# Operands moved to multiples of 512 and 1,024 bytes, and relu and square of three pairs in eight done by ScalarE

## The chip, the cores and the metric

The kernel runs on one core of a Trainium2 chip. The metric is the device time of one execution in microseconds (us); the median of three runs is given. A profile of one execution, taken by the hardware profiler, says what each engine did: PE is the matrix engine (PEld its weight loads), DVE is VectorE, ACT is ScalarE, POOL is GpSimd, and SP issues most of the transfers.

## The reference

A short causal convolution over the sequence (7 taps, softmax weights, one set for each of 8 heads) is followed by a two-layer network with an activation of three branches.

```python
def _attn_ref(x, weight):                     # x: 8 x 4096 x 192, weight: 8 x 7
    w = softmax(weight, axis=-1)
    x_pad = np.concatenate([np.zeros((B, pad, D)), x], axis=1)
    x_unf = x_pad[:, idx, :].reshape(B, S, K, H, group)
    return np.einsum('hk,bskhg->bshg', w, x_unf)

def _moe_ref(x, w_in, w_out):                 # x: 32768 x 192, w_in: 192 x 2048, w_out: 2048 x 192
    h = x @ w_in
    neg, pos = h <= -1, h >= 1
    g = np.where(pos, h, np.where(neg, 0.0, (h + 1) ** 2 / 4))
    return g @ w_out
```

## The kernel before, in words

**Tiles and steps.** The 32,768 rows are taken in 64 blocks of 512 (`s`, TB = 512), two blocks to a chunk `c`. The 2,048 hidden channels are 16 groups of 128, taken two at a time, so a block has 8 pairs (NPAIR = 8). The main loop (L830) runs over 512 pairs `q`, 8 to a block and 16 to a chunk; `i` is the pair's place in the chunk, 0 to 15. One turn of the loop is called a step here. In a step PE first does `mm1(q)`, the product with w_in for this pair, into one of two buffers `h` of PSUM, and then `mm2(q - 2)`, the product with w_out for the pair two steps back, which adds into four accumulators (`accm0`, `accm1`, `accr0`, `accr1`) that exist once.

**Precision.** From the second block on each product is made of three: weights and activations are split into a high part and a rest (`hi` and `lo`, `gh` and `gl`, type fp32r), and high by high, rest by high and high by rest are added up. Each matmul uses one half of the partitions (64 of 128), and the two halves run as a pair beside each other. `mm1` has 18 matmuls (9 pairs), `mm2` has 20 (10 pairs), so a step has 19 pairs of matmuls, all with 512 columns. The stationary operand of `mm1` and `mm2` is always 128 columns (512 bytes in a partition) of a weight tile `w2` to `w9` or `wr2` to `wr9`; the moving one is 512 columns (2,048 bytes) of an activation tile (`hi`, `lo`, `rh`, `rl`, `rhi`, `rlo`, `gh`, `gl`). The first block (s = 0) is done with plain float32 operands instead (L401 and `mm2_first`, L426), in whose products with w_out the activation is the stationary operand and 192 columns of the weights move.

**The activation.** For the pair q, `act_clip` (L460) has DVE clip h to -1 to 1 into a tile `g`, `act_square` (L466) has ACT square (g + 1) / 2 in place, and `act_max` (L471) has DVE take the larger of h and g. In the next step `act_hi` (L478) has ACT round g to `gh`, and `act_lo` (L483) has DVE subtract to `gl`. In the first block another form is in use: `both_square` (L745) has ACT do relu((h + 1) / 2) and then square it, and `most` (L752) has DVE take min(g, 1) and then the larger of that and h, in one instruction.

**Beside it.** When a block's last `mm2` has been issued, in the step with q mod 8 = 1, `evac` (L491) has ACT copy the four accumulators out; POOL adds them in pairs, and DVE transposes the sums for the store. The convolution of the next chunk runs in the same steps by a fixed plan (L697 to L705): transposes on DVE, products with the taps on ACT (`p`, `y`), their sums on POOL. Every engine takes its instructions in the order in which the program issues them; the schedule is manual.

**Where tiles stand.** Pools are laid out in each partition in the order in which they are opened, and tiles in a pool in the order in which they are first named, each rounded up to 32 bytes. The pool `const` begins at byte 16,512, which is 32 x 512 + 128. The weight tiles come first in it and all have sizes that are multiples of 512, so every weight tile starts at 128 modulo 512. Behind them come `wk` (56 bytes), `warm` (4), `whose` (1,120, of which 1,024 are used) and `ident` (512), then the pool `stage`, then `xin` with three tiles of 2,176 bytes, `xw` with two of 2,176 and five of 2,048, and then `xo`, `act` and `ob`, whose tiles are multiples of 1,024 bytes. By these sizes the tiles of `xo`, `act` and `ob`, the activations among them, all start at 448 modulo 1,024 (the first of them at byte 134,592).

Of the kernel before, what the change touches and what calls it, by code (L numbers as in the profile page):

```python
# [8 lines left out]
F32 = mybir.dt.float32  # L9
# [4 lines left out]
AF = mybir.ActivationFunctionType  # L14
# [4 lines left out]
P = 128  # L19
# [11 lines left out]
def lightconv_then_ffn(ctx: ExitStack, tc: tile.TileContext, x, weight, w_in, w_out, out):  # L31
# [24 lines left out]
    nc = tc.nc  # L56
    B, S, D = x.shape
    H, K = weight.shape
# [6 lines left out]
    NPAIR = NF // 2  # L65
# [5 lines left out]

    const = ctx.enter_context(tc.tile_pool(name="const", bufs=1))
    stage = ctx.enter_context(tc.tile_pool(name="stage", bufs=2))
    xin = ctx.enter_context(tc.tile_pool(name="xin", bufs=3))
    xw = ctx.enter_context(tc.tile_pool(name="xw", bufs=2))
    xo = ctx.enter_context(tc.tile_pool(name="xo", bufs=3))
    act = ctx.enter_context(tc.tile_pool(name="act", bufs=2))
    ob = ctx.enter_context(tc.tile_pool(name="ob", bufs=2))
    ps_h = ctx.enter_context(tc.tile_pool(name="ps_h", bufs=2, space=PSUM))
    ps_o = ctx.enter_context(tc.tile_pool(name="ps_o", bufs=1, space=PSUM))  # L80
    ctx.enter_context(tc.manual_schedule())
# [53 lines left out]
    class Conv:  # L135
# [133 lines left out]
        def split_halves(self):  # L269
# [26 lines left out]
    wo_w = w_out.bitcast(U32).rearrange("(f p) (d two) -> p f d two", p=P, two=2)  # L296
    n_in = [CI if j < NPAIR else 0 for j in range(NCH)]
    n_all = [n_in[j] + (CO if j >= LAG else 0) for j in range(NCH)]
    W = [const.tile([P, 2, n_in[j] + (CW if j >= LAG else 0)], F32R, name=f"w{j}")
         for j in range(NCH)]  # L300
    CC = max(n_all)
# [12 lines left out]
    class Chunk:  # L314
# [51 lines left out]
        def parts(self, rest):  # L366
            j, k = self.j, n_in[self.j]
            if rest:
                yield (WF[j][:, :, 0:P],
                       *(W[j][:, i, k:].rearrange("p (f d) -> p f d", f=2) for i in range(2)))  # L370
                yield WF[j][:, :, P:], WR[j][:, :, 0], WR[j][:, :, 1]
            else:
                yield WI[j], W[j][:, 0, 0:k], W[j][:, 1, 0:k]

# [11 lines left out]
    NQ = NSB * NPAIR  # L386
    WHOLE = (NF32 + 1,)
    hs, g32, gs, ghs, gls, accs = {}, {}, {}, {}, {}, {}

    def mm1(q):  # L390
# [11 lines left out]
        else:  # L402
            mms = [(W[j][:, part], u + u, [xop[s][u, x]] * 2) for u in "nsr"
                   for part, x in ((0, "hi"), (1, "hi"), (0, "lo"))]
# [25 lines left out]
    def mm2(q):  # L430

        s, j = divmod(q, NPAIR)
        gh, gl = ghs.pop(q), gls.pop(q)
        w, wr, k = W[j + LAG], WR[j + LAG], n_in[j + LAG]
        if j == 0:
# [21 lines left out]
    def tiles(q):  # L457
        return [slice(0, 1), slice(1, 2)] if q == NQ - 1 else [slice(0, 2)]

    def act_clip(q):  # L460
        g = gs[q] = act.tile([P, 2, TB], F32, name="g", bufs=3)
        for e in tiles(q):
            nc.vector.tensor_scalar(out=g[:, e, :], in0=hs[q][:, e, :], scalar1=-1.0, scalar2=1.0,  # L463
                                    op0=ALU.max, op1=ALU.min)

    def act_square(q):  # L466
        g = gs[q]
        for e in tiles(q):
            nc.scalar.activation(g[:, e, :], g[:, e, :], AF.Square, bias=0.5, scale=0.5)  # L469

    def act_max(q):  # L471
        h, g = hs.pop(q), gs[q]
        for e in tiles(q):
            nc.vector.tensor_tensor(out=g[:, e, :], in0=h[:, e, :], in1=g[:, e, :], op=ALU.max)  # L474
        if q < NF32:
            g32[q] = gs.pop(q)
# [90 lines left out]
                    in_=y[i][:, 0:2 * D].rearrange("p (b d) -> p b d", b=2))  # L567


    wk = const.tile([P, 2, K], F32, name="wk")  # L570
    warm = const.tile([P, 1], F32, name="warm")
    whose = const.tile([P, 2 * P + 3 * K + 3], F32, name="whose")[:, 0:2 * P]
    one = ob.tile([P, TB], F32, name="sum")[:, 0:P]
    small, busy = (ob.tile([P, TB // SQ, SQ], F32, name="osb").rearrange("p j b -> p (j b)")
                    for _ in range(2))
# [176 lines left out]
    def most(h, g):  # L752

        nc.vector.scalar_tensor_tensor(out=g, in0=g, scalar=1.0, in1=h, op0=ALU.min, op1=ALU.max)
# [75 lines left out]
    for q in range(NQ + DELAY):  # L830
# [22 lines left out]
        else:  # L853
# [6 lines left out]
            if q < NQ:  # L860
                let_go()
                act_clip(q)
                act_square(q)
# [6 lines left out]
            if q < NQ:  # L870
                let_go()
                act_max(q)
                parts_lo(q, (False,))
                conv_slot(i, conv_b, conv_n.get("a"), conv_n.get("r"))
# [38 lines left out]
```

## Time and profile before

| | us |
|---|---|
| median of three runs (2256.04 to 2256.80) | 2256.71 |
| span of the profiled execution, from its first instruction to its last | 2255.6 |
| what lies around the span: median less span | 1.1 |
| DVE, ACT and POOL busy in the span | 2103.2, 1697.6, 1168.4 |
| DVE busy, and ACT busy, in 16 steps in the middle (69.60 us) | 65.58, 52.88 |

The span is one execution; the median is that of other executions of the same kernel, and the two differ by what is spent before the first and after the last instruction. A busy time is the time in which an engine had an instruction in work. Idle time on an engine costs nothing as long as another one, which sets the end, does not wait for it.

### The profile page before, as it was taken

How to read it: one execution, taken by the hardware profiler on the slowest of the kernel's cores; microseconds unless marked ns; L12 is line 12 of the kernel's file. 1: busy time of each engine (PE TensorE's matmuls, PEld its weight loads, DVE VectorE, ACT ScalarE, POOL GpSimd, SP SyncE). 2: the span in 40 equal slices, each digit the busy share in tenths (PEclk: the TensorE clock that was granted, in tenths of full speed). 3: DMA queues.
4: the chain of work that ended last, by engine and by line, in shares of the span. 5: the costliest groups of instructions: out<-in, count | busy, mean ns of one | idle time of the engine just before them, and what ended most of it. 6: DMA issues, size and time to landing. Idle time of an engine off the chain costs nothing.

```text
span 2255.6 us, 48202 instructions
## 1 busy us (share of the span) xinstructions
PE 2249.6 (100%) x19645; PEld 1842.2 (82%) x19645; DVE 2103.2 (93%) x1883; ACT 1697.6 (75%) x2153; POOL 1168.4 (52%) x868
## 2 busy tenths in 40 slices
PE   9999999999999999999999999999999999999999
PEld 6988888888888888888888888888888888888887
DVE  8899999999999999999999999999999999999997
ACT  7677877778777787777877777877778777787775
POOL 1446644556445565454654455644556545565441
PEclk9999999999999999999999999999999999999999
DMA  7222222222222212222222222222222222212211
GB/s 158 49 51 48 42 46 47 51 53 39 51 49 46 53 34 51 49 49 51 41 46 47 49 51 51 39 49 46 49 53 39 51 49 46 54 35 50 49 34 24
DMA packets 442125, 110.84 MB, mean 49 GB/s; under 512 B 410288, under 2 KB 417840, under 8 KB 441904
## 3 DMA queue, kind: packets, MB, share of 16 engines
q1 hardware_dynamic: 441744, 107.66, 25.8%
q8 instruction: 155, 2.54, 0.5%
q14 instruction: 66, 0.54, 0.1%
q10 hardware_dynamic: 160, 0.10, 0.0%
HBM read 32.84 MB, written 25.17 MB: 26 GB/s over the span
## 4 chain that ended last, share of the span: by engine, by line
PE 100%; ACT 0%; DVE 0%; issue 0%; DVEq 0%; POOL 0%; POOLq 0%; ACTq 0%
PE h L408 47%; PE accm L452 30%; PE accr L452 20%; PE accr L426 1%; PE accm L426 1%; PE accr L190 0%; PE accm L602 0%; PE accr L408 0%; PE accm L181 0%; PE h L155 0%; PE h L553 0%; PE accr L646 0%; ACT xT L168 0%; ACT xT L165 0%; ACT xT L167 0%
## 5 line engine op out<-in xcount | busy, mean ns | idle before, releaser
L230 POOL TENSOR_TENSOR y<-y,p 128x512 f32<-128x512 f32 x546 | 765.5, 1402 | 730.8 <-DVE g L474 559.5
L487 DVE TENSOR_TENSOR gl<-g,gh 128x1024 fp32r<-128x1024 f32 (+1 forms) x497 | 732.1, 1473 | 27.6 <-ACT gh L481 23.6
L469 ACT ACTIVATE g<-g 128x1024 f32<-128x1024 f32 (+1 forms) x505 | 535.3, 1060 | 242.4 <-DVE g L463 232.9
L463 DVE TENSOR_SCALAR g<-h 128x1024 f32<-128x1024 f32 (+1 forms) x505 | 609.8, 1208 | 97.1 <-PE h L408 88.1
L481 ACT CAST gh<-g 128x1024 fp32r<-128x1024 f32 (+1 forms) x497 | 521.7, 1050 | 237.1 <-DVE g L474 225.6
L408 PE MATMUL h<-hi,w 64*128 64x512 f32 x4032 | 629.8, 389 | 0.0
L474 DVE TENSOR_TENSOR g<-h,g 128x1024 f32<-128x1024 f32 (+1 forms) x505 | 613.4, 1215 | 12.1 <-ACT g L469 4.5
L452 PE MATMUL accm<-gh,w 64*128 64x512 f32 x3966 | 535.0, 388 | 0.0
L408 PEld LDWEIGHTS h<-hi,w 64*128 64x128 f32 x4032 | 382.6, 184 | 81.9
L452 PEld LDWEIGHTS accm<-gh,w 64*128 64x128 f32 x3966 | 372.3, 184 | 81.8 <-issue 0.2
L408 PE MATMUL h<-lo,w 64*128 64x512 f32 x2016 | 399.6, 388 | 0.0
L219 ACT ACTIVATE p<-xT,wk 128x512 f32<-128x512 f32 x562 | 375.1, 710 | 0.0
L452 PE MATMUL accm<-gl,w 64*128 64x512 f32 x1984 | 308.1, 388 | 0.0
L452 PE MATMUL accr<-gl,wr 64*128 64x512 f32 x1984 | 308.0, 388 | 0.0
L452 PE MATMUL accr<-gh,wr 64*128 64x512 f32 x1984 | 308.0, 388 | 0.0
L408 PE MATMUL h<-rh,w 64*128 64x512 f32 x992 | 306.0, 388 | 0.0
L408 PE MATMUL h<-rhi,w 64*128 64x512 f32 x992 | 306.0, 388 | 0.0
L408 PEld LDWEIGHTS h<-lo,w 64*128 64x128 f32 x2016 | 193.3, 184 | 41.5 <-DMA lo<-lo 0.3
L501 POOL TENSOR_TENSOR sum<-t 128x512 f32<-128x512 f32 (+1 forms) x124 | 160.7, 1316 | 126.3 <-ACT t L499 126.3
L452 PEld LDWEIGHTS accm<-gl,w 64*128 64x128 f32 x1984 | 186.4, 184 | 40.9
L452 PEld LDWEIGHTS accr<-gh,wr 64*128 64x128 f32 x1984 | 186.4, 184 | 40.9
L452 PEld LDWEIGHTS accr<-gl,wr 64*128 64x128 f32 x1984 | 186.4, 184 | 40.9
(145 smaller groups left out, 1976.8 us busy)
## 6 DMA issues: line engine op xcount, KB each, us to landing
out_dram<-osb SPq DMA_DIRECT2D x366, 64.0 KB, 2.0
raw<-in_x_dram SPq DMA_DIRECT2D x334, 68.0 KB, 2.4
hi<-hi SPq DMA_DIRECT2D x126, 128.0 KB, 2.3
lo<-lo SPq DMA_DIRECT2D x126, 128.0 KB, 2.3
rhi<-rh SPq DMA_DIRECT2D x62, 128.0 KB, 2.2
rlo<-rl SPq DMA_DIRECT2D x62, 128.0 KB, 2.3
words<-in_moe_w_in_dram SPq DMA_DIRECT2D x16, 192.0 KB, 4.0
words<-in_moe_w_out_dram SPq DMA_DIRECT2D x8, 384.0 KB, 5.0
```

Source lines behind the costliest of these rows:

```text
L219: nc.scalar.mul(p, self.xT[:, SH + k:SH + k + TB], wk[:, self.wsel, k:k + 1])
L230: nc.gpsimd.tensor_add(y, y, self.product(k))
L408: nc.tensor.matmul(h[e], w[HALVES[e], c0:c0 + P], x[e][e], start=(n == 0), stop=(n == len(mms) - 1))
L426: nc.tensor.matmul(accs[s][a, i][:, c0:c0 + D], g[half, e, b * P:(b + 1) * P], w[half, e, :], start=(j == 0 and e == 0 and b % 2 == 0), st ...
L452: nc.tensor.matmul(accs[s][a, i], st, g[HALVES[i], e, :], start=(j == 0 and n == first[a]), stop=(j == NPAIR - 1 and n == last[a]))
L463: nc.vector.tensor_scalar(out=g[:, e, :], in0=hs[q][:, e, :], scalar1=-1.0, scalar2=1.0, op0=ALU.max, op1=ALU.min)
L469: nc.scalar.activation(g[:, e, :], g[:, e, :], AF.Square, bias=0.5, scale=0.5)
L474: nc.vector.tensor_tensor(out=g[:, e, :], in0=h[:, e, :], in1=g[:, e, :], op=ALU.max)
L481: nc.scalar.copy(gh[:, e, :], gs[q][:, e, :])
L487: eng.tensor_sub(gl[:, e, :], g[:, e, :], gh[:, e, :])
L501: nc.gpsimd.tensor_add(y[:, n], t[0][:, n], t[1][:, n])
```

## The change

It has two parts.

**Places.** `warm` is now the first tile of `const` and is given 320 bytes, of which the first element is used; `wk` follows (56 bytes, rounded to 64). So the weights begin at 16,512 + 320 + 64 = 16,896 = 33 x 512: every weight tile, and every slice of 128 columns that a matmul takes from it, starts at a multiple of 512. `whose` loses its padding. The pools `xw` and `xin`, whose tiles of 2,176 bytes are no multiple of 1,024, are opened last, so that `xo`, `act` and `ob` follow `stage` and all their tiles start at multiples of 1,024 (the first at 113,664 = 111 x 1,024). The tiles `xT`, `y`, `p` and `raw` of the two pools that are moved stand at multiples of 128. No instruction of PE is added, removed or moved by this.

**The activation.** For pairs with q mod 8 equal to 1, 4 or 6, from the third block to the last but one (q from 16 to 503, so 183 pairs), the form of the first block is used: ACT does relu and then square, and DVE does the one instruction of `most`. The clip on DVE goes.

```diff
     const = ctx.enter_context(tc.tile_pool(name="const", bufs=1))
     stage = ctx.enter_context(tc.tile_pool(name="stage", bufs=2))
-    xin = ctx.enter_context(tc.tile_pool(name="xin", bufs=3))
-    xw = ctx.enter_context(tc.tile_pool(name="xw", bufs=2))
     xo = ctx.enter_context(tc.tile_pool(name="xo", bufs=3))
     act = ctx.enter_context(tc.tile_pool(name="act", bufs=2))
     ob = ctx.enter_context(tc.tile_pool(name="ob", bufs=2))
+    xw = ctx.enter_context(tc.tile_pool(name="xw", bufs=2))
+    xin = ctx.enter_context(tc.tile_pool(name="xin", bufs=3))
...
+    warm = const.tile([P, 80], F32, name="warm")[:, 0:1]
+    wk = const.tile([P, 2, K], F32, name="wk")
     W = [const.tile([P, 2, n_in[j] + (CW if j >= LAG else 0)], F32R, name=f"w{j}")
          for j in range(NCH)]
...
+    def on_scalar(q):
+        return 2 * NPAIR <= q < NQ - NPAIR and q % NPAIR in (1, 4, 6)
+
     def act_clip(q):
         g = gs[q] = act.tile([P, 2, TB], F32, name="g", bufs=3)
+        if on_scalar(q):
+            nc.scalar.activation(g, hs[q], AF.Relu, bias=0.5, scale=0.5)
+            return
...
     def act_square(q):
         g = gs[q]
+        if on_scalar(q):
+            nc.scalar.activation(g, g, AF.Square)
+            return
...
     def act_max(q):
         h, g = hs.pop(q), gs[q]
+        if on_scalar(q):
+            most(h, g)
+            return
...
-    wk = const.tile([P, 2, K], F32, name="wk")
-    warm = const.tile([P, 1], F32, name="warm")
-    whose = const.tile([P, 2 * P + 3 * K + 3], F32, name="whose")[:, 0:2 * P]
+    whose = const.tile([P, 2 * P], F32, name="whose")
```

Two places show what moves. The first is ACT in the steps i = 8 and i = 9 of a chunk, up to the copies of the four accumulators. `gh<-g` is the rounding of the pair before, L248 a rounding for the convolution, L226 and L219 are products with taps. Before:

```order
L481 CAST gh<-g 128x1024
L469 ACTIVATE g<-g 128x1024
L248 CAST hi_5281<-y 128x512
L226 ACTIVATE y<-xT,wk 128x512
L219 ACTIVATE p<-xT,wk 128x512 x2
L481 CAST gh<-g 128x1024
L469 ACTIVATE g<-g 128x1024
L498 COPY t<-accm_4904 128x512
L499 COPY t<-accm_4905 128x512
L498 COPY t<-accr_4906 128x512
L499 COPY t<-accr_4907 128x512
```

In the changed kernel (its lines are numbered 8 to 14 higher here) the same place reads:

```order
L495 CAST gh<-g 128x1024
L480 ACTIVATE g<-g 128x1024
L248 CAST hi_5281<-y 128x512
L226 ACTIVATE y<-xT,wk 128x512
L219 ACTIVATE p<-xT,wk 128x512 x2
L495 CAST gh<-g 128x1024
L468 ACTIVATE g<-h 128x1024
L477 ACTIVATE g<-g 128x1024
L512 COPY t<-accm_4904 128x512
L513 COPY t<-accm_4905 128x512
L512 COPY t<-accr_4906 128x512
L513 COPY t<-accr_4907 128x512
```

The relu (L468) is new, and it stands between the rounding of g and the square, ahead of the copies that free the accumulators. The second place is DVE from the transpose that ends the step i = 7 to the transpose for the store in the step i = 10. Before:

```order
L147 STREAM_TRANSPOSE xT<-raw 128x544
L463 TENSOR_SCALAR g<-h 128x1024
L487 TENSOR_TENSOR gl<-g,gh 128x1024
L474 TENSOR_TENSOR g<-h,g 128x1024
L463 TENSOR_SCALAR g<-h 128x1024
L487 TENSOR_TENSOR gl<-g,gh 128x1024
L474 TENSOR_TENSOR g<-h,g 128x1024
L463 TENSOR_SCALAR g<-h 128x1024
L487 TENSOR_TENSOR gl<-g,gh 128x1024
L474 TENSOR_TENSOR g<-h,g 128x1024
L524 STREAM_TRANSPOSE osb<-sum 128x512
```

And in the changed kernel:

```order
L147 STREAM_TRANSPOSE xT<-raw 128x544
L471 TENSOR_SCALAR g<-h 128x1024
L501 TENSOR_TENSOR gl<-g,gh 128x1024
L488 TENSOR_TENSOR g<-h,g 128x1024
L501 TENSOR_TENSOR gl<-g,gh 128x1024
L766 SCALAR_TENSOR_TENSOR g<-g,h 128x1024
L471 TENSOR_SCALAR g<-h 128x1024
L501 TENSOR_TENSOR gl<-g,gh 128x1024
L488 TENSOR_TENSOR g<-h,g 128x1024
L538 STREAM_TRANSPOSE osb<-sum 128x512
```

In the step i = 9 the clip is gone and `most` (L766) stands where the maximum stood; the steps on either side are as they were.

## The prediction, made before the changed kernel ran

> **What bounds the kernel now.** I read the head of the page first, then the chain that ended last, then what PE waited for.
>
> ```profile
> span 2255.6 us, 48202 instructions
> PE 2249.6 (100%) x19645; PEld 1842.2 (82%) x19645; DVE 2103.2 (93%) x1883; ACT 1697.6 (75%) x2153; POOL 1168.4 (52%) x868
> PEclk9999999999999999999999999999999999999999
> PE 100%; ACT 0%; DVE 0%; issue 0%; DVEq 0%; POOL 0%; POOLq 0%; ACTq 0%
> ```
>
> PE is busy in the whole span at a full granted clock, and the chain lies on PE alone. A busy PE need not be PE at its best, so the waits of PE come next, and then the pace of its steps.
>
> ```profile
> PE accm L602 <- POOL osb L606: 1.2, 1, 1.2
> PE accr L190 <- ACT xT L168: 0.7, 1, 0.7
> PE h L553 <- DVE t L547: 0.2, 1, 0.2
> ...
> 1168.77 1.08 PE L452 MATMUL accm<-gh,w 64*128 64x512 f32 x8
> 1203.56 1.07 PE L452 MATMUL accm<-gh,w 64*128 64x512 f32 x8
> ```
>
> The three waits of PE add up to 2.1 us in all, at the two ends of the program. The two rows of the timeline are eight steps apart: 34.79 / 8 = 4.349 us a step, and with 19 pairs of matmuls in a step 0.2289 us a pair. In the main part, then, PE waits for nobody, and the time is the number of pairs times 0.2289. That number:
>
> ```profile
> L408 PE MATMUL h<-lo,w 64*128 64x512 f32 x2016 | 399.6, 388 | 0.0
> L452 PE MATMUL accr<-gl,wr 64*128 64x512 f32 x1984 | 308.0, 388 | 0.0
> ```
>
> Each of these stands four times in a step, so there are 504 steps with the new `mm1` (9 pairs) and 496 with the new `mm2` (10 pairs): 4,536 + 4,960 = 9,496 pairs, or 2,174 us of the span. What is left is the first block and the two ends.
>
> Is 0.2289 us the best a pair can do? The first block has pairs of the same shape with float32 operands, and others with 192 columns:
>
> ```profile
> 23.02 1.88 PE L408 MATMUL h<-hi,gh 64*128 64x512 f32 x8
> 24.73 1.02 PE L408 MATMUL h<-rh,gh 64*128 64x512 f32 x4
> 25.59 0.82 PE L426 MATMUL accm<-wf,g 64*128 64x192 f32 x8
> 26.24 0.82 PE L426 MATMUL accr<-wf,g 64*128 64x192 f32 x8
> ```
>
> From 23.02 to 25.59 there are six pairs of 512 columns, 0.4283 us each; from 25.59 to 26.24 four pairs of 192, 0.1625 us each. The 320 further columns cost 0.2658 us, so a column costs 0.83 ns and a pair 3 ns beside its columns. The fp32r pair takes a little over half of the float32 one. If a float32 operand costs exactly two columns' time where an fp32r one costs one (an estimate from these rows; nothing shows the two goes apart), the fp32r pair should take 512 x 0.415 + 3 = 0.2156 us. It takes 13.3 ns more, in every pair, whatever the other engines do. Over 9,496 pairs that is **126 us**.
>
> **The change part by part.** *Places.* PE's instructions stay as they are; only where their operands stand changes. So a pair's time can change only through the reading of operands, and no row of before has an fp32r pair at another place. I bound it: at best all of the 13.3 ns goes (-126 us); nothing may change (0); at worst the same excess comes a second time (+126 us). I take the first, since the nearest rows, the float32 pairs, read the same tiles without an excess, and since the excess is the same in all 19 pairs of a step, `mm1` and `mm2` alike, whose one common trait is the places: weights at 128 modulo 512, activations at 448 modulo 1,024. Against it speaks that the float32 pairs have no excess at those same places; they take twice as long over the same bytes, which would hide it.
>
> [...]
>
> *The activation.* The rows with the durations, the last three from the first block, where the new form is in use already:
>
> ```profile
> L474 DVE TENSOR_TENSOR g<-h,g 128x1024 f32<-128x1024 f32 x503 | 612.2, 1217 | 12.1 <-ACT g L469 4.5
> L463 DVE TENSOR_SCALAR g<-h 128x1024 f32<-128x1024 f32 x503 | 608.5, 1210 | 96.4 <-PE h L408 87.4
> L754 DVE SCALAR_TENSOR_TENSOR g<-g,h 128x1024 f32<-128x1024 f32 x7 | 8.5, 1215 | 0.0
> L749 ACT ACTIVATE g<-g 128x1024 f32<-128x1024 f32 x7 | 7.4, 1054 | 0.0
> L747 ACT ACTIVATE g<-h 128x1024 f32<-128x1024 f32 x7 | 7.1, 1021 | 2.3 <-PE h L408 2.3
> ...
> 1202.60:1272.20 69.60, 69.60 (x610) 57.06 (x610) 65.58 (x57) 52.88 (x66) 37.26 (x26) 1.00 0.26 47
> ```
>
> For each pair moved DVE loses the clip (1.21 us) and its other instruction costs the same; ACT gains the relu (1.02 us). Sixteen steps, 69.60 us now, hold six such pairs. With pairs of 0.2156 us they last 16 x 19 x 0.2156 = 65.5 us. DVE, busy for 65.58, would then have been the bound; it now has 65.58 - 6 x 1.21 = 58.3 (89%), and ACT 52.88 + 6 x 1.02 = 59.0 (90%). By load, both fit. By order one place is tight: the copies that free the accumulators stand behind the new relu. The rows from the end of `mm1(q)` at i = 8 to the next block's first `mm2`:
>
> ```profile
> 1168.77 1.08 PE L452 MATMUL accm<-gh,w 64*128 64x512 f32 x8
> 1168.97 1.22 DVE L463 TENSOR_SCALAR g<-h 128x1024 f32<-128x1024 f32 x1
> 1170.23 1.06 ACT L469 ACTIVATE g<-g 128x1024 f32<-128x1024 f32 x1 [0.88 <-DVE g L463]
> ...
> 1172.33 1.32 ACT L219 ACTIVATE p<-xT,wk 128x512 f32<-128x512 f32 x2
> 1173.56 1.04 ACT L481 CAST gh<-g 128x1024 fp32r<-128x1024 f32 x1
> 1174.58 1.06 ACT L469 ACTIVATE g<-g 128x1024 f32<-128x1024 f32 x1
> 1175.55 0.56 ACT L498 COPY t<-accm 128x512 f32<-128x512 f32 x1
> 1176.01 0.59 ACT L499 COPY t<-accm 128x512 f32<-128x512 f32 x1
> ...
> 1177.24 0.87 PEld L452 LDWEIGHTS accm<-gh,w 64*128 64x128 f32 x8
> 1177.47 1.07 PE L452 MATMUL accm<-gh,w 64*128 64x512 f32 x8
> ```
>
> ACT works without a pause from 1170.23 to the second copy's end at 1176.60, which is 7.83 us after 1168.77. PE wants both accumulators when the weight load begins: two steps later less 0.23, now 8.47 us. The relu adds some 0.95 us (instructions on ACT start a little before the last one ends: 0.97 from the square's start to the copy's, for a square of 1.06), so the copies end at 8.78. With faster steps PE wants them at 2 x 4.097 - 0.23 = 7.96, and waits 0.82 us. This place comes once in 16 steps, 30 times among the changed pairs: **25 us**. The other block end of a chunk (i = 1) has no such queue:
>
> ```profile
> 1207.52 1.05 ACT L481 CAST gh<-g 128x1024 fp32r<-128x1024 f32 x1
> 1209.43 1.06 ACT L469 ACTIVATE g<-g 128x1024 f32<-128x1024 f32 x1 [0.86 <-DVE g L463]
> ...
> 1210.86 0.59 ACT L499 COPY t<-accm 128x512 f32<-128x512 f32 x1
> ```
>
> There ACT stood idle for 0.86 us ahead of the square, waiting for the clip; the relu fills that gap, and the copies move from 7.89 us behind 1203.56 to about 7.98, which is when PE wants them. I cost it at nothing; if that cover fails, each 0.1 us there is 3 us. On DVE the relief at i = 4 and i = 6 shortens the wait of ACT for clips, so no backlog should reach i = 8. Bounds of this part: 0 (PE never waits) and 30 us.
>
> *The rest.* The first two blocks, the last one and the tail keep their instructions. Transfers start at other places; PE waited for none of them.
>
> **Sum**, against the span: 2255.6 - 126 + 25 = 2154.6 us, and with the 1.1 us around it 2156 us (4.5% faster than the median of 2256.71).
>
> **The rivals.** *The places don't matter to PE.* Steps stay at 4.349 us. PE wants the accumulators at 8.47 us, the copies end at 8.78: 0.31 us x 30 = 9 us, so **2266 us**, slower by 0.4%. The point from which this decides is the end of the second copy, 0.64 us of slack in the rows above; if the relu delays it by less, the time stays at 2257. For it: nothing in the trace ties the 13.3 ns to a place. Against it: no other engine's work disturbs the pair's time either, so something in the pair itself is left.
>
> *Part of the excess goes.* Half of it is 63 us; steps of 4.22 us leave a wait of 0.56 us x 30 = 17 us: **2210 us**.
>
> *The places get worse.* Weights and activations stand 320 bytes apart modulo 512 now, and 0 apart after; if the two readings disturb each other where they start alike, the excess grows. Doubled, it gives 2256.7 + 126 = **2383 us**; it is this case as soon as a pair takes over 0.229 us. No row speaks for it but the 13.3 ns themselves.
>
> **How the numbers follow.** Excess gone: 0.40, 2156 us, its own range 2125 (no wait, and 5 us for the pair's estimate) to 2170. Part of it gone: 0.24. Unchanged pairs: 0.22, of which 0.12 within 0.2% (about what can be told from no change here) and 0.10 slower. Worse: 0.14. Faster is 0.64, same 0.12, slower 0.24. The range leaves out the last case: 2125 to 2270.
>
> **What would show it.** Two rows of the first `accm<-gh` eight steps apart: 32.8 us if the excess is gone (33.3 with one wait of 0.8 among them), 34.8 if the places don't matter. A wait of PE or PEld for the copies of `accm` on ACT, some 30 times 0.8 us, would show the tight place; none would say that the queue on ACT was shorter than I worked out. DVE should fall by 183 x 1.21 = 221 us and ACT rise by 183 x 1.02 = 187 us. The forecast is wrong if the pair's time isn't near 0.2156, or if PE waits for g or h instead.

## The result, and the profile after

| | before | changed |
|---|---|---|
| median, us (4 runs each) | 2256.76 (2256.04 to 2258.71) | 2274.34 (2273.68 to 2276.06) |
| ratio to before, 95% interval | | 1.0078 (1.0063 to 1.0093) |
| span of the profiled execution, us | 2255.6 | 2273.2 |
| DVE, ACT busy, us | 2103.2, 1697.6 | 1898.1, 1861.6 |

The changed kernel is 17.6 us slower, 0.8%. The head of its page, and its chain that ended last:

```profile
span 2273.2 us, 47865 instructions
PE 2255.0 (99%) x19645; PEld 1932.4 (85%) x19645; DVE 1898.1 (83%) x1700; ACT 1861.6 (82%) x2336; POOL 1137.0 (50%) x868
PE 55%; ACT 20%; DVE 19%; issue 6%; POOL 0%; DVEq 0%; DMA 0%; SPq 0%; ACTq 0%; POOLq 0%
```

The chain lay on PE alone before; now 39% of it is on ACT and DVE. What PE and its weight loads waited for (total, times, longest):

```profile
PE accm L454 <- ACT t L512: 12.9, 29, 1.6
...
PEld accm L454 <- ACT t L512: 25.5, 30, 2.0
PEld accm L454 <- ACT t L513: 9.2, 30, 0.3
```

All of it is the place that the prediction called tight: the first `mm2` behind the copies at i = 9 waits for these (L512, L513), 30 times. The other block end of a chunk (i = 1), costed at nothing, shows no wait. The sum of these rows is no price, since a matmul and its weight load can wait in the same time (at 1186.38 both begin behind L512's copy, PE after 0.37 us and PEld after 0.79); the price comes from the runs below. Between the waits, steps are a little faster. Two rows four steps apart:

```profile
1199.70 0.39 PE L454 MATMUL accm<-gh,w 64*128 64x512 f32 x1
1216.93 0.39 PE L454 MATMUL accm<-gh,w 64*128 64x512 f32 x1
```

17.23 / 4 = 4.308 us a step, or 0.2267 us a pair, against 4.349 and 0.2289 before. (The eight matmuls of one row before stand in three rows now, at 1199.70, 1199.93 and 1200.61: behind a wait the two halves of a pair run out of step with each other.) So the places gained 2.2 ns a pair where 13.3 were forecast, and the wait cost more than the gain.

### The profile page after: what moved, and what is told of

Read it like the earlier page. It is cut to its first block, busy times and chain, and to the rows that moved or that the text cites. A ratio compares the mean times of both kernels' runs of the same rounds, so it can differ in the third digit from the quotient of the medians.

```text
span 2273.2 us, 47865 instructions
## 1 busy us (share of the span) xinstructions
PE 2255.0 (99%) x19645; PEld 1932.4 (85%) x19645; DVE 1898.1 (83%) x1700; ACT 1861.6 (82%) x2336; POOL 1137.0 (50%) x868
## 4 chain that ended last, share of the span: by engine, by line
PE 55%; ACT 20%; DVE 19%; issue 6%; POOL 0%; DVEq 0%; DMA 0%; SPq 0%; ACTq 0%; POOLq 0%
PE h L410 25%; PE accm L454 17%; PE accr L454 11%; DVE g L471 6%; DVE g L488 4%; ACT gh L495 4%; DVE gl L501 4%; ACT g L477 4%; ACT g L468 3%; ACT p L219 2%; DVE xT L147 2%; ACT y L226 2%; DVE g L766 2%; ACT g L480 1%; ACT hi L248 1%
## 5 line engine op out<-in xcount | busy, mean ns | idle before, releaser
L410 PE MATMUL h<-hi,w 64*128 64x512 f32 x4032 | 767.9, 387 | 0.0
L454 PE MATMUL accm<-gh,w 64*128 64x512 f32 x3966 | 655.1, 389 | 12.9 <-ACT t L512 12.9
L410 PE MATMUL h<-lo,w 64*128 64x512 f32 x2016 | 618.3, 386 | 0.0
L410 PEld LDWEIGHTS h<-hi,w 64*128 64x128 f32 x4032 | 565.5, 184 | 59.5
L480 ACT ACTIVATE g<-g 128x1024 f32<-128x1024 f32 x322 | 341.7, 1062 | 116.5 <-DVE g L471 108.9
L454 PE MATMUL accr<-gh,wr 64*128 64x512 f32 x1984 | 419.9, 387 | 0.0
L471 DVE TENSOR_SCALAR g<-h 128x1024 f32<-128x1024 f32 x322 | 386.9, 1202 | 33.4 <-PE h L410 33.0
L488 DVE TENSOR_TENSOR g<-h,g 128x1024 f32<-128x1024 f32 x322 | 391.4, 1216 | 4.5 <-ACT g L480 4.2
L410 PEld LDWEIGHTS h<-lo,w 64*128 64x128 f32 x2016 | 366.7, 184 | 29.6
L219 ACT ACTIVATE p<-xT,wk 128x512 f32<-128x512 f32 x562 | 375.8, 712 | 0.0
L766 DVE SCALAR_TENSOR_TENSOR g<-g,h 128x1024 f32<-128x1024 f32 x190 | 231.6, 1219 | 107.0 <-ACT g L477 106.9
```

What stands on the lines that cost most here:

```text
L219: nc.scalar.mul(p, self.xT[:, SH + k:SH + k + TB], wk[:, self.wsel, k:k + 1])
L410: nc.tensor.matmul(h[e], w[HALVES[e], c0:c0 + P], x[e][e], start=(n == 0), stop=(n == len(mms) - 1))
L454: nc.tensor.matmul(accs[s][a, i], st, g[HALVES[i], e, :], start=(j == 0 and n == first[a]), stop=(j == NPAIR - 1 and n == last[a]))
```

## The experiments

**Which part does what.** Four kernels. The first keeps the old activation (`on_scalar` is never true) at the new places:

```diff
-        return 2 * NPAIR <= q < NQ - NPAIR and q % NPAIR in (1, 4, 6)
+        return False
```

> The changed places alone, the activation as before. Theory: the places shorten each pair of fp32r matmuls from 0.2289 to 0.2266 us, and only the queue on ACT costs time; then a step is 4.305 us, no wait of PE on ACT is left, and the time is 2257 - 9,496 x 0.0023 = 2235 us. Rival: the shorter pair of the changed kernel came from its two halves running out of step with each other behind each wait, not from the places; then a step is 4.349 us and the time 2257 us.

The second has the new activation at the old places (the pools and the three tiles of `const` as before).

> Relu and square on ACT for the same 183 pairs, at the old places. Theory: pairs stay at 0.2289 us; PE waits for the copies of the accumulators at i = 9, about 1.0 us x 30 = 30 us (0.3 less a time than in the changed kernel, since steps are 0.044 us longer), so about 2287 us. Rival (halves out of step make the pair faster): pairs of 0.2266 us and about 2275 us, as the changed kernel.

The third and the fourth have the new places, with fewer pairs on ACT: without i = 9, and with i = 1 and i = 9 alone.

```diff
-        return 2 * NPAIR <= q < NQ - NPAIR and q % NPAIR in (1, 4, 6)
+        return 2 * NPAIR <= q < NQ - NPAIR and q % NPAIR in (1, 4, 6) and q % 16 != 9
...
-        return 2 * NPAIR <= q < NQ - NPAIR and q % NPAIR in (1, 4, 6)
+        return 2 * NPAIR <= q < NQ - NPAIR and q % NPAIR in (1,)
```

> The changed kernel without the pairs with i = 9 (five pairs of 16 on ACT in place of six). Theory: the wait of 1.3 us x 30 goes, since at i = 9 alone the queue ahead of the copies is long; 2235 to 2238 us. Rival: the backlog from i = 4 and i = 6 reaches the copies without the relu at i = 9 too, some 0.4 us x 30 = 12 us left: 2247 us.

> The changed kernel with the pairs with q mod 8 = 1 alone on ACT (i = 1 and i = 9; those at 4 and 6 are as before). Theory (the relu at i = 9 adds 0.95 us and a backlog from i = 4 and 6 the rest): waits of about 0.4 us x 30 = 12 us, so 2247 us. Rival (the relu at i = 9 alone makes the whole wait): 1.3 us x 30, so 2274 us.

| places | pairs on ACT | median, us | ratio to before, 95% interval |
|---|---|---|---|
| new | none | 2235.54 | 0.9906 (0.9892 to 0.9921) |
| old | i = 1, 4, 6, 9, 12, 14 | 2280.69 | 1.0107 (1.0090 to 1.0123) |
| new | i = 1, 4, 6, 12, 14 | 2237.86 | 0.9918 (0.9903 to 0.9932) |
| new | i = 1, 9 | 2247.23 (one run) | |
| new | i = 1, 4, 6, 9, 12, 14 (the change) | 2274.34 | 1.0078 (1.0063 to 1.0093) |

The kernel before had a median of 2256.86 us beside the first three. Two rows of steps with the new places and no pair on ACT, eight steps apart, and the waits of PE in that kernel:

```profile
1161.94 1.07 PE L454 MATMUL accm<-gh,w 64*128 64x512 f32 x8
1196.40 1.07 PE L454 MATMUL accm<-gh,w 64*128 64x512 f32 x8
...
PE accm L614 <- POOL osb L618: 1.2, 1, 1.2
PE accr L190 <- ACT xT L168: 0.4, 1, 0.4
PE h L567 <- DVE t L561: 0.2, 1, 0.2
```

34.46 / 8 = 4.308 us a step, with the halves in step and no wait in the main part. So the shorter pair comes from the places, and the rival (halves out of step) falls; it falls from the other side too, for at the old places, with waits, four steps still take 4.35 us each:

```profile
1163.39 1.18 PE L452 MATMUL accm<-gh,w 64*128 64x512 f32 x8
1180.79 1.19 PE L452 MATMUL accm<-gh,w 64*128 64x512 f32 x8
```

Out of step the pair is not shorter there (0.2289 us), and in places it is longer. In two stretches of that kernel, of six and eight steps, one half runs two pairs ahead of the other, and four steps without a wait take 17.73 us, 4.433 each (0.2333 a pair):

```profile
1021.89 0.39 PE L452 MATMUL accm<-gh,w 64*128 64x512 f32 x1
1039.62 0.39 PE L452 MATMUL accm<-gh,w 64*128 64x512 f32 x1
```

The places alone are worth 21.3 us (9,496 pairs x 2.2 ns = 20.9). The new activation costs 2274.3 - 2235.5 = 38.8 us at the new places, 1.29 us for each of the 30 steps with i = 9, and 23.8 us, 0.79 each, at the old ones, where steps are slower and PE wants the accumulators later. I had expected 30 us there; the size was off, the sign not. Without the relu at i = 9 only 2.3 us of the 38.8 are left; with it, but without those at i = 4 and 6 (and 12 and 14), 11.7 us, 0.39 each. So the large wait needs both: the relu ahead of the copies, and work that is already late when it gets there. The fastest version here is the one with the places alone; no moved pair is needed with it, since its steps of 4.308 us still hide DVE, busy for 65.23 of 68.90 us in 16 of them:

```profile
1161.94:1230.84 68.90, 68.90 (x610) 56.95 (x608) 65.23 (x57) 52.74 (x67) 37.61 (x27) 1.00 0.25 48
```

**Which operand's place.** All of these have the old activation, so PE waits for nobody and the time is the pair's time. The tiles are shifted by the padding of `warm` and `whose` and by the order of the pools, as in these two edits (weights and activations both at 128, where `xin` is opened last as well; weights at multiples of 512 and activations 64 past multiples of 1,024):

```diff
-    whose = const.tile([P, 2 * P + 3 * K + 3], F32, name="whose")[:, 0:2 * P]
+    whose = const.tile([P, 2 * P + 40], F32, name="whose")[:, 0:2 * P]
...
-    whose = const.tile([P, 2 * P], F32, name="whose")
+    whose = const.tile([P, 2 * P + 16], F32, name="whose")[:, 0:2 * P]
```

> Activation form as before; weights at multiples of 512 bytes, activations left at 448 modulo 1,024. If the place of the stationary operand makes the pair shorter: 0.2267 us a pair and 2235.5 us. If that of the moving operand does: 0.2289 us and 2257 us. If each gives a part: between, near 0.2278 us and 2246 us.

> Activation form as before; weights left at 128 modulo 512, activations at multiples of 1,024. The mirror image: 0.2289 us a pair and 2257 us if the stationary operand's place counts, 0.2267 us and 2235.5 us if the moving one's does, between if each gives a part.

> The kernel before without the 96 bytes of padding behind one tile: weights at 128 modulo 512, activations at 352 modulo 1,024, so 32 past a multiple of 64. If the moving operand's place counts by how many blocks of 64 bytes or more it touches, the pair gets longer than 0.2289 us, by 1 ns or more (2266 us or more); if only the weights' place counts, 0.2289 us and 2257 us.

> The changed places without the new activation form, with the pool of the raw weights moved behind the activations, so that the tiles of 2,048 and 4,096 bytes start at multiples of 2,048 rather than at 1,024 modulo 2,048. If a moving operand that crosses a multiple of 2,048 costs time: under 0.2267 us a pair and under 2234 us; if 1,024 is all that counts, or the place of the moving operand doesn't: 0.2267 us and 2235.5 us.

The first two came out as none of the theories had it: each half of the change alone is slower than the kernel before, by 1.84% (1.69 to 2.00) and 1.43% (1.26 to 1.60). Steps with weights at 512 and activations at 448, and with weights at 128 and activations at 0, eight apart in each:

```profile
1163.20 1.10 PE L454 MATMUL accm<-gh,w 64*128 64x512 f32 x8
1198.66 1.10 PE L454 MATMUL accm<-gh,w 64*128 64x512 f32 x8
```

```profile
1163.13 1.10 PE L452 MATMUL accm<-gh,w 64*128 64x512 f32 x8
1198.45 1.10 PE L452 MATMUL accm<-gh,w 64*128 64x512 f32 x8
```

35.46 / 8 = 4.433 us (0.2333 a pair) and 35.32 / 8 = 4.415 (0.2324). No single operand's place makes the gain; the two act together. The other two: with activations at 352 the time is 2299.2 us, longer as its first theory had it, and with activations at multiples of 2,048 it is 2235.4, so these bring nothing beyond 1,024. Next I tried the distance between the two operands, moving less stationary, modulo 256.

> Activation form as before; weights at 128 modulo 512 and activations at 128 modulo 1,024: no distance between the two starts, but neither at a multiple of 512. Theory (the distance of moving and stationary operand modulo 256 sets the pair; so far 0: 0.2267, 64: 0.2289, 128: 0.2324, 192 and 224: 0.2333 us): 0.2267 us a pair, 2235.5 us. Rival (each operand has to start at a multiple of 512 or more, as in the change): more than 0.2289 us, 2257 us or above.

> Weights at multiples of 512, activations 64 past multiples of 1,024. By the distance modulo 256: 0.2289 us a pair and 2257 us, as the kernel before, whose distance is 320. By alignment: some 0.233 us and 2297 us, as with activations at 448.

> Weights at multiples of 512, activations 256 past multiples of 1,024. If the distance counts modulo 256: 0.2267 us a pair and 2235.5 us. If it counts modulo 512 or more, or if activations have to stand at multiples of 512: longer, up to 0.2333 us and 2298 us.

> Weights at multiples of 512, activations 32 past multiples of 1,024. If the pair grows evenly with the distance: between 0.2267 and 0.2289 us, some 2246 us. If it goes in blocks of 64 bytes: 0.2267 us or 0.2289 us. Below 0.2267 us would say that the change's place is not the best one.

All kernels with the old activation, sorted by that distance (the pair from steps eight apart, the two halves in step; medians of several runs for the kernel before, the places alone, 512 with 448 and 128 with 0, one run each for the rest):

| weights mod 512 | activations mod 1,024 | distance mod 256 | pair, us | time, us |
|---|---|---|---|---|
| 0 | 0 (the change) | 0 | 0.2267 | 2235.5 |
| 0 | 0 (multiples of 2,048) | 0 | 0.2267 | 2235.4 |
| 0 | 256 | 0 | 0.2267 | 2235.5 |
| 128 | 128 | 0 | 0.2267 | 2235.4 |
| 0 | 32 | 32 | 0.2333 | 2298.6 |
| 128 | 448 (before) | 64 | 0.2289 | 2256.8 |
| 0 | 64 | 64 | 0.2289 | 2256.8 |
| 128 | 0 | 128 | 0.2324 | 2289.7 |
| 0 | 448 | 192 | 0.2333 | 2298.9 |
| 128 | 352 | 224 | 0.2333 | 2299.2 |

Two pairs of rows settle it. Weights and activations both at 128 are as fast as the change, though neither is at a multiple of 512; and activations 64 past multiples of 1,024, with weights at multiples of 512, give the time of the kernel before to 0.1 us, though both operands stand elsewhere. Of the last four expectations the distance was right in the first three. The fourth (a distance of 32) came out of neither form of it: not between 0 and 64, but at the top, as 192 and 224.

## Why the prediction was wrong, point by point

**What bounds the kernel** was right: the time before is 9,496 pairs at 0.2289 us and two ends, with no wait of PE in the main part, and in the kernels without waits the time moves with the pair alone (2.2 ns less a pair, 21 us less; 4.4 ns more, 42 us more).

**The term for the places failed in size:** -126 us was forecast, -21 was measured. The step that failed is the one that took all 13.3 ns above the float32 rows for an effect of the places. Only 2.2 of them are, at the places of the change. The other 11 ns are there in all ten layouts; 0.2267 us is the shortest pair seen, and what makes it longer than the estimate of 0.2156 stays open, the estimate itself included: that a float32 operand costs exactly two columns' time where an fp32r one costs one was my assumption, and no run shows it. The argument from "the one common trait" was weak: whatever belongs to every fp32r pair is common to all of them. The other argument rested on a misreading: the float32 pairs of 512 columns don't read the same tiles. Both their operands are activation tiles (`hi` and `gh` in the row at 23.02), at a distance of 0 modulo 256 in every layout; only the float32 pairs of 192 columns read a weight tile.

**The rival "the places don't matter to PE"** (2266 us) fell with the places alone at 0.9906, though its time is the nearest of all to the measured one; that is luck. **"The places get worse"** had it the wrong way round: at a distance of 0 the pair is the shortest of those tried (0.2267 us), not the longest, and the longer pair that I feared is what either half of this change brings alone (0.2333 and 0.2324 us). That two readings disturb each other was a supposition; no run shows it. **"Part of the excess goes"** was what happened to the pair, a sixth of it rather than half.

**The term for the activation failed too.** It was worked out as 0.82 us x 30 for steps of 4.097 us. For the steps of 4.308 us that the pairs really gave, the same working has PE want the accumulators at 2 x 4.308 - 0.23 = 8.39 us and the copies end at 8.78: 0.39 us x 30 = 12 us. Measured: 1.29 us x 30.

With i = 1 and 9 alone on ACT it is 0.39 us, as worked out, but by two errors that cancel. In that kernel the second copy ends 9.01 us behind `mm1` at i = 8, and not 8.78:

```profile
1163.78 1.29 PE L454 MATMUL accm<-gh,w 64*128 64x512 f32 x8
...
1172.20 0.59 ACT L513 COPY t<-accm 128x512 f32<-128x512 f32 x1
```

Yet 9.01 costs only 0.37 us at most places, and without the relu at i = 9, where the trace has it end at 8.71, a place costs under 0.1 (2.3 us over 30 places is 0.08). So PE loses time from some 8.6 us on (an estimate: 9.01 less 0.37 is 8.64, 8.71 less 0.08 is 8.63), which is two steps, and not from the start of the weight load at 8.39.

In the changed kernel what failed is the sentence that the relief of DVE at i = 4 and 6 lets no backlog reach i = 8. ACT there, from the rounding at i = 5 to that at i = 7:

```profile
1165.35 1.03 ACT L495 CAST gh<-g 128x1024 fp32r<-128x1024 f32 x1
1166.29 1.06 ACT L480 ACTIVATE g<-g 128x1024 f32<-128x1024 f32 x1
1167.25 0.60 ACT L248 CAST hi<-y 128x512 fp32r<-128x512 f32 x1
1167.75 1.33 ACT L219 ACTIVATE p<-xT,wk 128x512 f32<-128x512 f32 x2
1168.99 1.03 ACT L495 CAST gh<-g 128x1024 fp32r<-128x1024 f32 x1
1169.93 1.01 ACT L468 ACTIVATE g<-h 128x1024 f32<-128x1024 f32 x1
1170.98 1.06 ACT L477 ACTIVATE g<-g 128x1024 f32<-128x1024 f32 x1
1171.94 1.32 ACT L219 ACTIVATE p<-xT,wk 128x512 f32<-128x512 f32 x2
1173.33 1.05 ACT L495 CAST gh<-g 128x1024 fp32r<-128x1024 f32 x1
```

None of these rows has an idle time ahead of it: ACT works through two steps without a pause. What that does to DVE, and then to the copies (PE's row at 1176.99 is the end of `mm1(q)` at i = 8; DVE's go from the subtraction at i = 7 to the clip at i = 8):

```profile
1174.41 2.15 DVE L501 TENSOR_TENSOR gl<-g,gh 128x1024 fp32r<-128x1024 f32 x1
1176.48 1.21 DVE L488 TENSOR_TENSOR g<-h,g 128x1024 f32<-128x1024 f32 x1
1177.62 0.73 DVE L147 STREAM_TRANSPOSE xT<-raw 128x544 f32<-128x544 f32 x1
1178.28 1.18 DVE L471 TENSOR_SCALAR g<-h 128x1024 f32<-128x1024 f32 x1
...
1176.99 0.39 PE L454 MATMUL accm<-gh,w 64*128 64x512 f32 x1
...
1186.23 0.59 ACT L513 COPY t<-accm 128x512 f32<-128x512 f32 x1
...
1186.38 1.68 PE L454 MATMUL accm<-gh,w 64*128 64x512 f32 x8 [0.37 <-ACT t L512]
```

The subtraction can't begin before the rounding ends at 1174.38, and takes 2.15 us; the maximum and the transpose stand behind it; so the clip at i = 8 begins 1.29 us behind `mm1`, where it was 0.20 before. With this 1.09 us and the relu's 0.95 on top of the 7.83 us of before the copies should end at 9.87; they end at 1186.82, 9.83 us behind `mm1`.

Most of the 1.09 us is the subtraction itself, and the prediction had no term for its length. At the same place before it took 1.21 us:

```profile
1165.77 1.21 DVE L487 TENSOR_TENSOR gl<-g,gh 128x1024 fp32r<-128x1024 f32 x1
```

With i = 1 and 9 alone on ACT it took 1.3 us in nearly all chunks, against 2.1 in nearly all of the changed kernel's. In the changed kernel's trace none of the 191 subtractions of this shape that ran while POOL stood idle took over 1.23 us; the longer ones, up to 2.35, all ran beside an addition on POOL. Not every one that did was long (of the 304 that ran beside an instruction on POOL 81 took 1.25 us or less, and the one of before, just shown, ran beside additions too), so what decides it is not shown. By load the two engines fitted, as forecast (1861.6 and 1898.1 us busy of 2273.2); the wait comes from order and lateness in six steps of 16.

The 1.29 us are a mean. In the profiled execution 27 of the 30 places cost 1.1 to 1.2 us, the first 0.5, and two some 3.9. At these two PE stood for 1.56 and 1.59 us instead of 0.4, and 1.2 to 1.4 us after it went on the granted clock fell to 0.50 for 3.4 us, which costs some 1.7 us each time (an estimate: half of 3.4). The first of them, with a stretch that lies inside the 3.4 us (its clock is the third value from the end):

```profile
834.53 1.95 PE L454 MATMUL accm<-gh,w 64*128 64x512 f32 x8 [1.56 <-ACT t L512]
...
836.00:839.00 3.00, 3.00 (x18) 2.39 (x16) 2.62 (x3) 3.00 (x4) 1.98 (x3) 0.50 0.00 0
```

Nowhere else in the main part did the clock fall. Whether the long wait brings it down is not shown.

**What the profile was to show:** a wait for the copies of `accm` some 30 times was there, mostly at 1.1 to 1.2 us, 1.29 in the mean, and not 0.8. DVE fell by 205 us (221 forecast) and ACT rose by 164 (187). The time, 2274.3, is 4 us above the range's upper end of 2270: the range had the unchanged pair with waits as worked out, and not the backlog.

## What to carry to other kernels

Where PE is the bound and never waits, the pace of its pairs is worth comparing across placements of the operands, by their distance rather than by their alignment (0.2267 to 0.2333 us a pair here); moving one of two operands to a rounder address cost 1.4% and 1.8% here, and moving both gained 0.9%. Work that is moved to an engine because its mean load allows it is paid where it stands in the queue: count the steps before the tight one as well, since a queue that is full there arrives late, and an instruction that comes to run at another time can take longer (the subtraction at i = 7 took 2.15 us in place of 1.21). Time the parts of a change apart; here a gain of 21 us hid under a loss of 39.

## What the runs showed of the hardware

- An fp32r pair of 512 columns took 0.2267, 0.2289, 0.2324 or 0.2333 us, and with its two halves in step which one followed from the distance of its moving operand's start from its stationary operand's, modulo 256 bytes: 0, 64, 128 and 192 in that order, with 32 and 224 at 0.2333. Other distances weren't tried, and why it is so is open.
- The float32 pairs of 192 columns in the first block show nothing of it. Their moving operand is a weight tile and their stationary one an activation tile, so their distance is 192 before, 0 in the change, 64 with activations at 448 and 224 with activations at 32 (weights at multiples of 512 in these two); four pairs take 0.65 us in all four. The float32 pairs of 512 columns stand at a distance of 0 everywhere and can't show it. The row of the kernel with activations at 32 (a distance of 224 here), and the next one of the same kind:

```profile
25.22 0.82 PE L428 MATMUL accm<-wf,g 64*128 64x192 f32 x8
25.87 0.82 PE L428 MATMUL accr<-wf,g 64*128 64x192 f32 x8
```

- After a wait the two halves of a pair stayed out of step with each other for many steps: in the changed kernel for all 15 steps from 137.46 us, behind the first wait, to the next wait at 202.83. At the new places the pace of a step stayed the same (4.308 us); at the old ones, with the new activation, it was 4.35 us, and 4.433 in the two stretches where one half ran two pairs ahead. So at the old places the distance alone doesn't fix the pair.
- In the changed kernel a subtraction on DVE (`gl`, 128 x 1024) took 1.20 to 1.23 us with POOL idle, and 1.20 to 2.35 us beside an instruction on POOL; what decides it is not shown.
- The granted clock of PE fell to 0.50 for 3.4 us, 1.2 to 1.4 us after the end of each of the two waits of over 1.5 us (1.56 and 1.59) in the main part of the changed kernel.
